# An early pair's epsilon: added by ScalarE as the bias of a copy instead of by VectorE in an operation of its own

## The chip, the core and the metric

The kernel runs on one core of a Trainium2 chip. The core has a matrix engine (PE), a vector engine (DVE), a scalar engine (ACT), a general engine (POOL) and a queue engine (SP) that here issues all transfers between the memory of the chip (HBM) and the core's own memory (SBUF). PE writes its results to a second small memory, PSUM, from which DVE and ACT read. Each engine works through its own list of instructions in order, and waits on semaphores where an instruction needs something from another engine.

The metric is the device time of one execution in microseconds (us), taken as the median of several runs. Before the change it is 964.43 us (three runs, 964.29 to 965.21).

## What is computed

Attention with a block-causal mask over 8 batches of 8 heads (576 positions, head size 64), and then a gated MLP on the 4608 rows that it gives, all in float32:

```python
scores = scale * np.matmul(q, k.transpose(0, 1, 3, 2))
scores = np.where(mask, scores, -1000000000.0)      # block_i >= block_j, blocks of 64
scores = scores - np.max(scores, axis=-1, keepdims=True)
attn = np.exp(scores)
attn = attn / (np.sum(attn, axis=-1, keepdims=True) + 1e-09)
x = np.matmul(attn, v)                              # rows: batch and position, columns: head and size
h = (x @ w1) * (x @ w2) @ w3
out = h @ w_out
```

The 1e-9 in the fifth line is what the change is about.

## The kernel before

**Pairs.** The work of the attention is cut into 32 pairs of heads (4 pairs to a batch). A pair has two heads, `j` = 0 and 1, which share the partitions: head 0 has partitions 0 to 63, head 1 has 64 to 127. For each head the scores are made transposed, in five tiles (`s_tile`, L281, PE writes `s`), ACT takes the exponential (L289 for pairs 0 to 3, the **early** pairs; L296 to L301 for the others), and PE multiplies with the values (L321 early, L345 later, both write `x`).

**The shift.** Ahead of a pair's scores the maxima of its score blocks are found (`shift_mask`: PE L206 writes `mx`, DVE L213 reduces it to `m`, PE L217 transposes `m` to `mt`, ACT L219 writes `ms` with the sign turned). A small transfer (L228) puts `ms` as an extra row into the operand `qk`, one for each head. So the second half of every score tile waits for that transfer. `mt` and `ms` of pair 4 are made while pair 3 is still at work.

**Operands.** `prep_qk` puts the two heads' queries and keys into `qk`, each split into a high and a low part: ACT casts the high part (L251), a transfer copies it to the other partitions (L255), DVE subtracts to get the low part (L258).

**Row sums of an early pair.** The values of an early pair (`ve`) have 64 columns of ones beside the values, so the product `x` holds the row sums on the other head's partitions. ACT copies these out of PSUM to `sm` (L370) and the values to `x32` (L371). `norm` then has a short chain on DVE: reduce `sm` with a transpose to `rr` (L381), add 1e-9 (L382), take the reciprocal (L383), spread it by a transpose to `rb` (L385), multiply into `xr` (two pieces, L392). `rr` has 128 x 18 elements. The later pairs add 1e-9 in another place (`total`, L364), which stays as it is.

**Weights.** Beside pairs 0 to 3 the kernel prepares the weights of the MLP. They arrive as 20 tiles of 1 MB that hold float64 numbers; ACT (L168) and DVE (L169, L170, L171) assemble float32 from them, and for `w1` and `w2` ACT and DVE split each into a high and a low part (L184, L185). PE multiplies `w3` with `w_out` once (`gen_product`, L461), and ACT and DVE split that product (L464, L465). Three buffers `wraw` take the tiles.

**Later stage.** From pair 4 on the attention and the MLP run side by side: ACT casts `xr` to `xh` (L405), POOL makes the rest `xl` (L406), PE multiplies (L481, L499).

**What sets the order.** The first instructions, and all of PE's from pair 4 on, stand in the order in which the code is written. For the rest, and for all engines during pairs 0 to 3, a scheduler orders each engine's list when the kernel is built, with costs of its own for every instruction. So a change of one operation in the early pairs can move others that it has nothing to do with. All lists are fixed once the kernel is built.

Of the kernel before, what the change touches and what calls it, by code (L numbers as in the profile page):

```python
# [7 lines left out]
F32 = mybir.dt.float32  # L8
# [3 lines left out]
AF = mybir.ActivationFunctionType  # L12
# [4 lines left out]
P = 128  # L17
# [60 lines left out]
def block_causal_attention__then__gated_mlp_kernel(ctx, tc, qkv, consts, ident_in, w1, w2, w3t, wout, out_t):  # L78
    nc = tc.nc
    w1, w2, w3t, wout = (w.bitcast(I32) for w in (w1, w2, w3t, wout))  # L80

    cpool = ctx.enter_context(tc.tile_pool(name="cpool", bufs=1))
# [24 lines left out]
    tl = {}  # L107
# [5 lines left out]
    def load_qk(n):  # L113
        t = raw_pool(n).tile([P, RQK], F32, tag="rqk", name=f"rqk{n}")
        for cols in (slice(S, 2 * S), slice(0, S)) if n == 0 else (slice(0, RQK),):
            nc.sync.dma_start(out=t[:, cols], in_=qkv[n // NPAIR, n % NPAIR][:, cols])
        rqk_of[n] = t

    def load_v(n):
        t = raw_pool(n).tile([P, RV], F32, tag="rv", name=f"rv{n}")  # L120
        nc.sync.dma_start(out=t, in_=qkv[n // NPAIR, n % NPAIR][:, RQK:])
        rv_of[n] = t
# [3 lines left out]
    start.enter_context(tc.manual_schedule(engines={ET.PE, ET.DVE, ET.Activation, ET.SP, ET.Pool}))  # L126
    load_qk(0)
    nc.gpsimd.memset(qd, 0.0)
    nc.sync.dma_start(out=both, in_=ident_in)
    load_v(0)  # L130
    wstack = ExitStack()
# [234 lines left out]
    def take_early(n, j, xps, x32, rr):  # L366
        o, x = own[j], oth[j]
        if j == 0:
            tl["sm"] = work.tile([P, S], F32, tag="tr", name=f"sm{n}")
        nc.scalar.copy(tl["sm"][o], xps[x, 384:960])  # L370
        nc.scalar.copy(x32[o], xps[o, 384:960])  # L371

    def take(n, j, xps, x32):
# [5 lines left out]
    def norm(n, x32, rr):  # L379
        if n < EARLY:  # L380
            nc.vector.tensor_reduce(rr, tl["sm"].rearrange("p (b c) -> p b c", c=32), axis=AX.X, op=ALU.max, apply_transpose=True)  # L381
            nc.vector.tensor_scalar_add(rr, rr, 1e-9)  # L382
        nc.vector.reciprocal(rr, rr)  # L383
        rb = work.tile([P, S], F32, tag="tr", name=f"rb{n}")
        nc.vector.transpose(rb, rr.unsqueeze(2).broadcast_to([P, S // 32, 32]))  # L385
        b, c = divmod(n, NPAIR)
        for k in (b, b + 1):
            lo, hi = max(k * TB, b * S), min((k + 1) * TB, (b + 1) * S)
            if (k, c) not in x_of:
                x_of[k, c] = xpool.tile([P, TB], F32, tag=f"x{c}", name=f"xr{k}_{c}")  # L390
            sl = slice(lo - b * S, hi - b * S)
            (nc.vector if n < EARLY else nc.gpsimd).tensor_tensor(out=x_of[k, c][:, lo - k * TB : hi - k * TB], in0=x32[:, sl], in1=rb[:, sl], op=ALU.mult)  # L392
        done_x.add((b, c))
        split_ready()
# [4 lines left out]
    def split_ready():  # L399
        k = st["free"]  # L400
        for c in range(NC):
            if "xh" in tl and k < NTB and (min(k, B - 1), c) in done_x and (k, c) not in st["split"]:
                st["split"].add((k, c))
                src = x_of[k, c]
                nc.scalar.copy(tl["xh"][c], src)  # L405
                nc.gpsimd.tensor_tensor(out=tl["xl"][c], in0=src, in1=tl["xh"][c], op=ALU.subtract)  # L406
# [133 lines left out]
    def pair(n):  # L540
# [9 lines left out]
        for j in range(2):  # L550
# [4 lines left out]
            for step in (FIRST_PLANS[n] if n < len(FIRST_PLANS) else PLAN)[j].split():  # L555
# [6 lines left out]
                with tc.high_priority(offset=0) if early else nullcontext():  # L562
                    if step == "S":
                        s_tile(n, j, next(tiles), p_early)
                    elif step == "F":
                        fill(mlp, 1)
                    elif step == "M":
                        fill(masks, 1)
                    elif step == "A":
                        fill(next_qk, 1)  # L570
                    elif step == "B":
                        fill(own_qk, 1)
                        steps_b += 1
                        if steps_b == 2 and n >= EARLY and not last:
                            load_qk(n + 1)
                    elif step == "V":
                        fill(pvs, 1)
                    elif step == "R":
                        sums(n, j, part)
                    elif step == "N" and early:  # L580
                        take_early(n, j, xps, x32, rr)
                    elif step == "N":
                        take(n, j, xps, x32)
                    elif step == "T":
                        if not early:
                            total(n, part, rr)
                        norm(n, x32, rr)
                    elif step == "Q" and not last:
                        if n + 1 != NPAIR:
                            prep_v(n + 1, j)  # L590
                        if j == 1 and n + 2 <= EARLY:
                            load_qk(n + 2)
                        if j == 1 and n + 2 < NN and n + 1 != NPAIR:
                            load_v(n + 2)
# [66 lines left out]
```

## Time and profile before

| | |
|---|---|
| median of 3 runs | 964.43 us (964.29 to 965.21) |
| the profiled execution's own time | 962.94 us |
| its span, first to last instruction | 961.2 us |
| ACT copies of `sm` (L370) in it | 8, of 626 to 638 ns |
| ACT copies of `x32` (L371) | 8, of 632 to 636 ns |

The profile is of one execution. Its first part gives the busy time of each engine and its share of the span. A timeline row gives start and duration in us, engine, line, operation, what it writes and reads, the shape, how many instructions were merged (x), and in brackets how long the engine had been idle before it and what ended that. "SPq" is the queue engine issuing a transfer. Where instructions follow each other closely the printed durations overlap by some hundredths. A table of stretches gives, for each stretch of time, the busy time of each engine with the number of its instructions, then the clock that PE was granted (1.00 is full speed), the busy share of the DMA engines and what they moved.

### The profile page before, as it was taken

The numbers are of one execution on the slowest core, as the hardware profiler recorded it, in microseconds if no ns is written. First come the engines' busy times: TensorE is split into PE (matmuls) and PEld (weight loads), VectorE is DVE, ScalarE is ACT, GpSimd is POOL, SyncE is SP. The second block draws the span as 40 slices with busy tenths as digits, with TensorE's granted clock in tenths as the row PEclk, the third lists the DMA queues.
The fourth block names the chain that finished last, engine by engine and source line by source line (L and its number), as shares of the span: only waits on it lengthen the run. The fifth ranks groups of instructions, "written<-read, shape, count | busy, mean of one in ns | idle before, by whom it ended". The sixth has DMA issues, their size and how long they took to land.

```text
span 961.2 us, 13354 instructions
## 1 busy us (share of the span) xinstructions
PE 937.1 (97%) x4580; PEld 749.9 (78%) x4608; DVE 609.5 (63%) x1289; ACT 565.9 (59%) x1274; POOL 304.5 (32%) x254
## 2 busy tenths in 40 slices
PE   5999979999999999999999999999999999999998
PEld 3455557888888888888888888888888888888886
DVE  6999977766776677766776777667776776210010
ACT  5776766666666666666666666666666665222121
POOL 0000043442335334533453334333443443223120
PEclk9999979999999999999999999999999999999999
DMA  8897334445445544455445544554455442000001
GB/s 256 299 285 237 108 79 94 114 118 142 113 113 124 145 113 113 113 146 124 111 94 143 124 105 107 135 132 106 106 130 129 106 111 60 22 1 33 12 1 44
DMA packets 48823, 111.68 MB, mean 116 GB/s; under 512 B 5866, under 2 KB 14186, under 8 KB 48756
## 3 DMA queue, kind: packets, MB, share of 16 engines
q1 hardware_dynamic: 48756, 110.84, 44.7%
q8 instruction: 36, 0.59, 0.3%
q14 instruction: 31, 0.25, 0.1%
HBM read 50.51 MB, written 9.44 MB: 62 GB/s over the span
## 4 chain that ended last, share of the span: by engine, by line
PE 90%; DVE 3%; ACT 3%; DMA 2%; issue 1%; POOL 0%; SPq 0%; ACTq 0%; DVEq 0%
PE ab L481 42%; PE o L499 20%; PE s L281 10%; PE x L345 9%; PE mx L206 3%; PE w L461 3%; PE x L321 2%; DMA rqk<-in_qkv 1%; DMA wraw<-in_w 1%; DVE m L213 1%; DVE wbits L170 0%; ACT qk L251 0%; PE tot L362 0%; DVE qk L258 0%; ACT pe L289 0%
## 5 line engine op out<-in xcount | busy, mean ns | idle before, releaser
L489 POOL TENSOR_TENSOR gl<-a,gh 128x512 fp32r<-128x512 f32 x72 | 93.7, 1301 | 239.3 <-ACT gh L488 236.2
L281 PE MATMUL s<-qk 128*128 128x288 f32 (+4 forms) x768 | 158.8, 312 | 9.5 <-DMA qk<-ms 4.7
L281 PEld LDWEIGHTS s<-qk 128*128 128x128 f32 (+1 forms) x768 | 125.8, 183 | 42.5 <-issue 8.9
L213 DVE TENSOR_REDUCE m<-mx 128x1 f32<-128x512 f32 (+6 forms) x256 | 125.4, 503 | 34.0 <-PE mx L206 26.2
L300 ACT ACTIVATE ph<-s 128x448 fp32r<-128x448 f32 x224 | 85.9, 383 | 70.4 <-PE s L281 63.6
L481 PE MATMUL ab<-xh,w2h 128*128 128x512 f32 x288 | 126.4, 439 | 0.0
L271 POOL TENSOR_TENSOR vs<-rv,vs 128x320 fp32r<-128x320 f32 x56 | 48.9, 874 | 233.4 <-ACT vs L270 233.4
L499 PE MATMUL o<-gh,wh 128*128 128x512 f32 x288 | 117.3, 407 | 0.0
L487 DVE TENSOR_TENSOR a<-ab,a 128x512 f32<-128x512 f32 x72 | 49.6, 688 | 106.6 <-PE ab L481 103.9
L302 DVE TENSOR_TENSOR pl<-s,ph 128x448 fp32r<-128x448 f32 x168 | 81.4, 484 | 54.9 <-ACT s L301 54.3
L481 PE MATMUL ab<-xh,w1h 128*128 128x512 f32 x288 | 114.5, 397 | 0.1
L298 DVE TENSOR_TENSOR pl<-rsum,ph 128x288 fp32r<-128x288 f32 x112 | 56.7, 530 | 90.4 <-ACT ph L297 90.2
L481 PE MATMUL ab<-xl,w2h 128*128 128x512 f32 x288 | 113.3, 393 | 0.0
L481 PE MATMUL ab<-xl,w1h 128*128 128x512 f32 x288 | 113.3, 393 | 0.0
L481 PE MATMUL ab<-xh,w1l 128*128 128x512 f32 x288 | 113.0, 392 | 0.0
L499 PE MATMUL o<-gl,wh 128*128 128x512 f32 x288 | 112.9, 392 | 0.0
L481 PE MATMUL ab<-xh,w2l 128*128 128x512 f32 x288 | 112.6, 391 | 0.0
L499 PE MATMUL o<-gh,wl 128*128 128x512 f32 x288 | 112.6, 391 | 0.0
L243 POOL TENSOR_TENSOR rqk<-rqk,hf 128x1152 fp32r<-128x1152 f32 x27 | 72.2, 2673 | 90.8 <-ACT hf L240 90.8
L303 DVE TENSOR_TENSOR rsum<-s,rsum 128x448 f32<-128x448 f32 x224 | 92.7, 414 | 1.7
L345 PE MATMUL x<-ph,vs 128*128 128x128 f32 x336 | 87.2, 312 | 0.0
L301 ACT ACTIVATE s<-s 128x448 f32<-128x448 f32 x224 | 85.1, 380 | 0.0
(76 smaller groups left out, 1730.9 us busy)
## 6 DMA issues: line engine op xcount, KB each, us to landing
qk<-hf SPq DMA_DIRECT2D x108, 288.0 KB, 3.1
rqk<-in_qkv SPq DMA_DIRECT2D x31, 576.0 KB, 4.7
qk<-rqk SPq DMA_DIRECT2D x54, 288.0 KB, 4.8
rv<-in_qkv SPq DMA_DIRECT2D x32, 320.0 KB, 2.9
out_t<-o SPq DMA_DIRECT2D x36, 256.0 KB, 2.0
wraw<-in_w3t SPq DMA_DIRECT2D x8, 1024.0 KB, 5.6
wraw<-in_w SPq DMA_DIRECT2D x8, 1024.0 KB, 6.7
wraw<-in_wout SPq DMA_DIRECT2D x4, 1024.0 KB
```

Of the source, the lines that this page charges most:

```text
L213: nc.vector.reduce_max(m[:, col : col + 1], sc, axis=AX.X)
L243: nc.gpsimd.tensor_tensor(out=lo, in0=rqk_of[n], in1=hf, op=ALU.subtract)
L281: nc.tensor.matmul(t[ks, at : at + q1 - q0], qk[j][:, 2 + s, kr], qk[j][:, s, q0:q1], start=(s == 0), stop=(s == 1))
L298: nc.vector.tensor_tensor(out=low, in0=r, in1=h, op=ALU.subtract)
L300: nc.scalar.activation(h, sc, AF.Exp, scale=SCALE)
L301: nc.scalar.activation(sc, sc, AF.Exp, scale=SCALE)
L302: nc.vector.tensor_tensor(out=low, in0=sc, in1=h, op=ALU.subtract)
L303: nc.vector.tensor_tensor(out=r, in0=sc, in1=r, op=ALU.add)
L345: nc.tensor.matmul(xps[:, to : to + w], v[:, c, :], parts[s][:, a : a + w], start=(u < 2 and s == 0), stop=((u, s) in ((0, 1), (len(PV) - ...
L481: nc.tensor.matmul(acc[i], l[:, c, fs], r[c], start=(c == 0 and s == 0), stop=(c == NC - 1 and s == 2))
L489: nc.gpsimd.tensor_tensor(out=gl[f // 4][:, f % 4], in0=a32, in1=gh[f // 4][:, f % 4], op=ALU.subtract)
L499: nc.tensor.matmul(t, l[:, f, es], r[f // 4][:, f % 4], start=(f == 0 and s == 0), stop=(f == NF - 1 and s == 2))
```

## The change

ScalarE's copy of the row sums becomes an activation with the identity function and a bias, which is a column of a small tile `eps` that POOL fills with 1e-9 at the start. VectorE's addition in `norm` is gone. The copies are 8 (two for each early pair), the additions were 4.

```diff
     nc.gpsimd.memset(qd, 0.0)
+    eps = cpool.tile([P, 32], F32, name="eps")
+    nc.gpsimd.memset(eps, 1e-9)
     nc.sync.dma_start(out=both, in_=ident_in)
...
         if j == 0:
             tl["sm"] = work.tile([P, S], F32, tag="tr", name=f"sm{n}")
-        nc.scalar.copy(tl["sm"][o], xps[x, 384:960])
+        nc.scalar.activation(tl["sm"][o], xps[x, 384:960], AF.Identity, bias=eps[x, 0:1])
         nc.scalar.copy(x32[o], xps[o, 384:960])
...
             nc.vector.tensor_reduce(rr, tl["sm"].rearrange("p (b c) -> p b c", c=32), axis=AX.X, op=ALU.max, apply_transpose=True)
-            nc.vector.tensor_scalar_add(rr, rr, 1e-9)
         nc.vector.reciprocal(rr, rr)
```

No instruction is added or lost beside these and POOL's one memset; the scheduler, however, puts the early pairs' instructions into another order from the end of pair 0 on. Line numbers of the changed kernel are higher by 2 from the second memset to `norm`, and by 1 behind it. From pair 4 on all five lists hold the same instructions in the same order as before, but for what is shown here and for ACT's cast of pair 3's `xr` to `xh`, which now stands behind pair 4's first two exponentials instead of ahead of them. Three places show what moved. In the rows below, numbers in a name are those of the tile, or tell the head (`s_1`) and the pair's turn.

The first place is DVE's list at the end of pair 0, where its chain `rr` stands among the assembly of weights. Before:

```order
L171 SCALAR_TENSOR_TENSOR wo_112<-wraw,wbits 128x1024
L169 TENSOR_SCALAR wbits<-wbits 128x1024
L382 TENSOR_SCALAR rr_185<-rr_185 128x18
L258 TENSOR_TENSOR qk_87<-rqk_173,qk_87 64x1152
L170 SCALAR_TENSOR_TENSOR wbits<-wraw,wbits 128x1024
L465 TENSOR_TENSOR wl<-w_204,wh 128x512
L171 SCALAR_TENSOR_TENSOR w_334<-wraw,wbits 128x1024
```

The same place of DVE's list in the changed kernel:

```order
L173 SCALAR_TENSOR_TENSOR wo_114<-wraw,wbits 128x1024
L171 TENSOR_SCALAR wbits<-wbits 128x1024
L384 RECIPROCAL rr_187<-rr_187 128x18
L172 SCALAR_TENSOR_TENSOR wbits<-wraw,wbits 128x1024
L386 STREAM_TRANSPOSE rb_378<-rr_187 128x576
L466 TENSOR_TENSOR wl<-w_206,wh 128x512
L173 SCALAR_TENSOR_TENSOR w_336<-wraw,wbits 128x1024
```

The reciprocal has moved up, some 10 instructions ahead of where it stood, and the spreading transpose with it; the subtraction for `qk_87` (L258, pair 1's second head) has moved out of this piece, to a place some 17 instructions later.

The second place is ACT's list at the end of pair 3, where the last exponentials of the early stage (`pe`), the cast of pair 4's second head (`qk_87`), pair 3's copies (`sm`, `x_3`), pair 4's shift (`ms`) and its values (`vs`) follow each other. Before:

```order
L184 CAST w2h_89<-wbits 128x1024
L289 ACTIVATE pe_1_843<-s_1_878 128x192
L289 ACTIVATE pe_1_843<-s_1_878 64x64
L251 CAST qk_87<-rqk_730 64x2x576
L370 COPY sm_834<-x_1_842 64x576
L371 COPY x_3_761<-x_1_842 64x576
L219 ACTIVATE ms_903<-mt_901 9x128
L270 CAST vs_934<-rv_732 128x5x64
```

The same place of ACT's list in the changed kernel:

```order
L186 CAST w2h_89<-wbits 128x1024
L291 ACTIVATE pe_1_842<-s_1_855 128x448
L291 ACTIVATE pe_1_842<-s_1_868 128x320
L291 ACTIVATE pe_1_842<-s_1_877 128x192
L291 ACTIVATE pe_1_842<-s_1_877 64x64
L221 ACTIVATE ms_902<-mt_900 9x128
L253 CAST qk_87<-rqk_730 64x2x576
L372 ACTIVATE sm_833<-x_1_841,eps 64x576
L373 COPY x_3_760<-x_1_841 64x576
```

`ms` now stands ahead of the cast of `qk_87` and of both copies, where it stood behind all three; and the cast of the weights `w2h` stands ahead of two exponentials that it stood behind. SP's list follows: the transfers of pair 4's `ms` into both heads' operands now come ahead of the copy of `qk_87` (L257), which stands behind the loading of the next values.

The third place is PE's list at the same time: the last products of pair 3 (`x_1`), pair 4's transpose `mt`, and the first scores of pair 4 (`s_0`). Before:

```order
L206 MATMUL mx_5_893<-kb_796,qd 128x64
L281 MATMUL s_0_962<-qk_86 128x288
L321 MATMUL x_1_842<-pe_1_843,ve_170 128x192
L321 MATMUL x_1_842<-pe_1_843,ve_170 128x64
L217 MATMUL mt_901<-ident,m_800 9x128
L281 MATMUL s_0_962<-qk_86 128x288
L481 MATMUL ab<-xh_926,w1h_80 128x512
```

The same place of PE's list in the changed kernel:

```order
L283 MATMUL s_1_877<-qk_87 64x64 x2
L219 MATMUL mt_900<-ident,m_799 9x128
L283 MATMUL s_0_960<-qk_86 128x288
L323 MATMUL x_1_841<-pe_1_842,ve_172 128x192
L323 MATMUL x_1_841<-pe_1_842,ve_172 128x64
L283 MATMUL s_0_960<-qk_86 128x288
L482 MATMUL ab<-xh_924,w1h_80 128x512
```

The transpose `mt` now stands ahead of pair 3's last two products, where it stood behind them. What follows the second `s_0` is the same in both.

## The prediction

> **What bounds the kernel now.** The page comes first, then a table of stretches: the early stage (24 to 124 us, pairs 0 to 3 beside the weights; the 24 us ahead of it keep their order), the change of stage, and the rest.
>
> ```profile
> span 961.2 us, 13354 instructions
> PE 937.1 (97%) x4580; PEld 749.9 (78%) x4608; DVE 609.5 (63%) x1289; ACT 565.9 (59%) x1274; POOL 304.5 (32%) x254
> ```
>
> ```profile
> 24.00:124.00 100.00, 96.23 (x337) 51.47 (x336) 96.24 (x134) 71.49 (x117) 0.00 (x0) 1.00 0.71 223
> 124.00:134.00 10.00, 4.60 (x13) 3.11 (x12) 9.29 (x10) 6.98 (x16) 7.28 (x6) 0.65 0.44 123
> 134.00:961.00 827.00, 823.28 (x4194) 687.99 (x4221) 487.43 (x1124) 473.56 (x1123) 295.39 (x241) 1.00 0.41 99
> ```
>
> From 134 us on PE is busy 823 of 827 us, and its list is the same in both kernels: what happens earlier shifts that block as a whole. So the question is when PE gets to 134 us. In the early stage DVE and PE are each busy 96 of 100 us. Nearly all that the change touches is there, or in the 10 us behind it, where PE is busy less than half the time and runs at a granted clock of 0.65.
>
> DVE's waits in the early stage are few:
>
> ```profile
> DVE m L213 <- PE mx L206: 1.2, 2, 1.0
> DVE w1l L185 <- ACT w1h L184: 0.8, 1, 0.8
> DVE qk L258 <- ACT qk L251: 0.4, 1, 0.4
> DVE wbits L169 <- ACT wbits L168: 0.4, 2, 0.2
> DVE rr L381 <- ACT sm L370: 0.3, 1, 0.3
> ```
>
> The change of stage is read from the timeline, all engines together:
>
> ```profile
> 123.21 1.15 ACT L251 CAST qk<-rqk 64x1152 fp32r<-64x1152 f32 x1
> 123.70 0.13 DVE L215 TENSOR_REDUCE m<-m 128x1 f32<-128x2 f32 x1
> 124.02 0.28 PE L217 MATMUL mt<-ident,m 128*9 128x128 f32 x1
> 124.27 0.63 ACT L370 COPY sm<-x 64x576 f32<-64x576 f32 x1
> 124.39 1.35 DVE L258 TENSOR_TENSOR qk<-rqk,qk 64x1152 fp32r<-64x1152 f32 x1 [0.56 <-ACT qk L251]
> 124.92 0.63 ACT L371 COPY x<-x 64x576 f32<-64x576 f32 x1
> 125.58 0.27 ACT L219 ACTIVATE ms<-mt 9x128 fp32r<-9x128 f32 x1
> 125.78 0.78 DVE L381 TRANSPOSE_TENSOR_REDUCE rr<-sm 128x18 f32<-128x576 f32 x1
> 125.87 0.82 ACT L270 CAST vs<-rv 128x320 fp32r<-128x320 f32 x2
> 126.40 1.68 POOL L271 TENSOR_TENSOR vs<-rv,vs 128x320 fp32r<-128x320 f32 x2 [124.00 <-ACT vs L270]
> 126.59 0.70 DVE L382 TENSOR_SCALAR rr<-rr 128x18 f32<-128x18 f32 x1
> 127.33 0.27 DVE L383 RECIPROCAL rr<-rr 128x18 f32<-128x18 f32 x1
> 127.63 0.78 DVE L385 STREAM_TRANSPOSE rb<-rr 128x576 f32<-128x576 f32 x1
> 128.04 5.63 POOL L406 TENSOR_TENSOR xl<-xr,xh 128x512 fp32r<-128x512 f32 x4
> 128.25 0.61 PE L281 MATMUL s<-qk 128*128 128x288 f32 x1 [3.95 <-DMA qk<-ms]
> 128.51 2.57 DVE L392 TENSOR_TENSOR xr<-x,rb 128x512 f32<-128x512 f32 x2
> 129.51 0.66 PE L481 MATMUL ab<-xl,w1h 128*128 128x512 f32 x1
> 131.16 2.83 DVE L298 TENSOR_TENSOR pl<-rsum,ph 128x288 fp32r<-128x288 f32 x2
> 134.05 0.74 PE L345 MATMUL x<-pl,vs 128*128 128x448 f32 x1 [0.97 <-DVE pl L298]
> ```
>
> PE idles 3.95 us until the transfer of `ms` has landed (128.25), and its last wait of all is for the second `pl` of DVE, at **134.05**. DVE reaches `pl` through its own chain (L258, L381, L382, L383, L385, `xr`), without a pause. So what ends last at the change of stage is DVE's chain, not the transfer.
>
> **What the change removes.** Four additions. Their group, and a pair of `xr` from the middle of the stage for comparison:
>
> ```profile
> L382 DVE TENSOR_SCALAR rr<-rr x4: 157/170/703, 41.9 to 126.6; 128x18 f32<-128x18 f32 x4
> 106.85 0.82 DVE L392 TENSOR_TENSOR xr<-x,rb 128x512 f32<-128x512 f32 x2
> ```
>
> Three take about 0.17 us each, together at most 0.5 us of a DVE that is 96% busy. The last one took 0.70 us, and its successor started 127.33 - 126.59 = 0.74 us after it. It lay beside POOL's `vs` (126.40 to 128.08); a pair of `xr` likewise took 2.57 us beside POOL's `xl`, against 0.82 us without POOL. So the long time was a wait for POOL, and it goes with the instruction: **-0.74 us** on DVE's chain.
>
> **What it adds.** Eight copies get a bias. The trace has no copy with a bias column; the nearest row is the same copy without one (0.63 us, at 124.27). I take nothing for the bias: per element the same work. The bounds are zero and the whole copy again, 0.63 us, of which only pair 3's second copy can lie on the last chain. ACT is busy 71 of 100 us in the stage, so the other seven are covered; without that cover they would cost as many times the same. POOL's memset lies at the start, where POOL has nothing to do until 126.40; the first copy needs it some 20 us later.
>
> The Trainium skill speaks against the change here: "ScalarE: Activation LUTs", section "What ACT_TABLE_LOAD costs", says that an operand which points to a column of 128 values adds about 93 ns to an activation. As an estimate from that page this is eight times 0.09 us on ACT and 0.09 us on the last chain; the sum would be 0.1 us higher. No run here shows it yet.
>
> **What it moves, in the middle of the stage.** The order rows of the first place put `wl` (L465) right behind the transpose.
>
> ```profile
> 41.88 0.16 DVE L382 TENSOR_SCALAR rr<-rr 128x18 f32<-128x18 f32 x1
> 43.43 1.23 DVE L170 SCALAR_TENSOR_TENSOR wbits<-wraw,wbits 128x1024 int32<-128x1024 int32 x1
> 43.64 0.59 ACT L464 CAST wh<-w 128x512 fp32r<-128x512 f32 x1
> ```
>
> It would come up at 41.88 + 0.27 + 1.23 + 0.78 (reciprocal, L170, transpose) = 44.16 us by the printed durations, which overlap a little, so at about 43.95, while what it reads is cast until 44.23. So one wait of about 0.3 us is new, beside the 0.5 us that went. Further on others go and come: the waits shown above sum to 3.1 us and can at best all vanish, with the additions -3.6 us; new ones of the largest size shown, 1.0 us, at two places would make +2. ACT carries both risks: casts (`wh`, `w2h`) now stand ahead of exponentials that PE waits for. I take **0** for the middle, since the pieces I can name cancel within 0.2 us.
>
> **What it moves, at the change of stage.** ACT now does `ms` first. It needs `mt`, which PE ends at 124.30 as before (124.02 plus 0.28; it needs `m`, not PE's products). So `ms` runs at 124.34 instead of 125.58, and the transfer lands **1.24 us earlier**, at about 127.0. But the cast of `qk` (L251), which was over at 124.36, now begins at about 124.6 and ends at about 125.75: **+1.4 us** for DVE's L258, which waits for it, and for all that is queued behind L258 on DVE. With the 0.74 us gone, `xr` starts 0.66 us later than before, at about 129.16. On ACT the copies of `sm` and `x` and then `vs` follow the cast, so `vs` begins at about 127.1, 1.2 us later; POOL's `vs` then ends at 129.3 instead of 128.08 and its `xl` follow. Who gets ahead there decides. If `xr` comes before the first `xl`, the second `pl` ends about 0.66 us later than before. If `xl` comes first, as in this trace, DVE waits for each `xl` in turn, and the whole of POOL's delay, 1.2 us, and about one part of its L406 (5.63/4 = 1.4 us, less what `xr` itself takes) stand in the way: at most +1.9 us. The two starts differ by 0.1 us, so I cannot say which; between 0.66 and 1.9, I take **+1.0 us**, nearer to DVE's own chain, because that is the row that ends last. PE's first scores are earlier by 1.2 us, but it meets `xl` (129.51 before, at 130.6 or later now) and then `pl`, so nothing of that remains. SP's queue: the copy of `qk` now stands behind the loading of values, which waits for POOL's `vs` (about 129.3); it is needed for the second head, whose scores begin beyond 140 us, and the next load behind it slips by under 1 us.
>
> Sum, for the profiled execution: 962.94 us = 961.2 span + 1.7 around it; 0 in the middle, +1.4 - 0.74 + 0.3 for POOL = +1.0, gives 963.9. That execution lay 1.5 us below the median of the runs, so for the median: 964.43 + 1.0 = **965.4 us**.
>
> **The rivals.** The clock matters for two of them:
>
> ```profile
> 123.60:127.00 3.40, 0.70 (x4) 0.38 (x3) 2.78 (x5) 3.33 (x7) 0.60 (x1) 1.00 0.38 84
> 127.00:130.40 3.40, 2.15 (x6) 1.57 (x6) 3.23 (x5) 1.74 (x4) 3.40 (x4) 0.50 0.36 98
> 130.40:133.85 3.45, 2.15 (x7) 1.45 (x5) 3.37 (x3) 2.31 (x7) 3.28 (x3) 0.50 0.55 178
> 133.85:137.25 3.40, 3.20 (x11) 2.87 (x12) 2.10 (x5) 1.89 (x4) 0.00 (x0) 0.50 0.00 0
> 137.25:140.65 3.40, 3.40 (x18) 2.90 (x18) 1.23 (x5) 2.63 (x7) 0.85 (x1) 1.00 0.00 0
> ```
>
> After a stretch with 0.70 us of PE work the clock was halved, for three stretches of 3.4 us; two with 2.15 us of work did not end that, one with 3.20 us did. PE lost half of what lay behind 134.05: (137.25 - 134.05)/2 = 1.6 us.
>
> *Slower: half speed for one stretch more.* If PE's dense work begins 1.0 us later, the stretch that ends at 137.25 holds about 2.2 us of it, no more than those that did not end it. Half speed would last until 140.65: +1.0 and +1.7 = 967.1. It decides where the dense work starts more than about half a microsecond into a stretch; against it, stretches need not lie the same in each run.
>
> *Faster: the clock is not halved.* `mt`, the last products and the early scores break PE's idle time of 3.95 us into pieces. If that keeps the clock up, -1.6 + 1.0 = -0.6: 963.8. Against it: PE then waits for `xl`, so another stretch is as empty.
>
> This is the rule of the Trainium skill, "TensorE: Matmul & The Clock Gate", section "Part 1: The HAM clock gate (the "warmup" mystery)": the clock goes by activity in free-running windows of 3413 ns, one idle window halves it, one busy one restores it. The trace agrees, with three stretches of 3.4 us.
>
> *Faster: the stage ends earlier.* DVE's waits shrink in the new order by more than the new ones add, about 1 of the 3.1 us, while POOL costs nothing: -1.0 - 0.5 + 0.66 = -0.8: 963.6. DVE's 96% speak for it; PE's 96% beside it against.
>
> *No effect at all.* The casts and PE hide both: 964.4; a special case of the forecast.
>
> **How the numbers follow.** Forecast (964.4 to 966.2, with no effect at its low end) 0.55; half speed longer 0.20; clock kept 0.10; stage earlier 0.15. The range 963.2 to 967.2 leaves out about half of the cases that end lowest and the slower rival's upper part. 0.2% is 1.93 us, about what a measurement can tell from no change: faster means below 962.5, slower above 966.4. Faster: the unlikely ends of the last two cases, 0.08; slower: most of the 0.20 and the forecast's upper end, 0.25; within: 0.67.
>
> **What would show it.** Right: `ms` ahead of L251 by about 1.2 us earlier, L258 of pair 4's second head some 1.4 us behind the final `m` more than before, no 0.70 us row in DVE's chain, and PE's last wait for `pl` near 135. Wrong: `pl` no longer the last wait, the clock at 1.00 between 127 and 137 us, or a stage whose end (the final `m`, 123.70 before) moves by more than 1 us either way.

## The result, and the profile after

The changed kernel takes **970.66 us** (median of 6 runs, 968.02 to 973.1), beside 964.66 us for the kernel before in the same comparison (6 runs). The ratio is 1.0068, with a 95% interval from 1.0053 to 1.0083: slower by 6.0 us. The prediction, 965.4 us with a range of 963.2 to 967.2, is missed.

The page of the changed kernel's profiled execution (970.38 us, against 962.94 before) begins:

```profile
span 968.6 us, 13378 instructions
...
PE 944.1 (97%) x4608; PEld 750.2 (77%) x4608; DVE 607.9 (63%) x1285; ACT 566.4 (58%) x1274; POOL 304.3 (31%) x255
```

The span grew by 7.4 us, and PE's busy time by 7.0. The same three stretches as in the prediction, the last one to 968 us, where before it ended at 961 (columns: stretch, length, busy time and instructions of PE, PEld (PE's loading of weights), DVE, ACT and POOL, PE's clock, DMA share, GB/s):

```profile
24.00:124.00 100.00, 95.88 (x336) 50.69 (x335) 96.96 (x132) 72.11 (x118) 0.00 (x0) 1.00 0.70 224
124.00:134.00 10.00, 5.71 (x16) 3.63 (x17) 7.68 (x9) 8.03 (x17) 6.62 (x6) 0.62 0.37 105
134.00:968.00 834.00, 830.89 (x4221) 689.22 (x4221) 487.85 (x1124) 473.15 (x1123) 295.73 (x242) 1.00 0.40 98
```

The third row holds what nobody touched: 4221 weight loads, as before, at full clock but for its start, and PE busy for 830.89 us where it was 823.28. So the loss lies in the part whose list of instructions is the same.

It does not come from a late start. These rows are the change of stage in the changed kernel, from the timeline:

```profile
123.44 0.28 PE L219 MATMUL mt<-ident,m 128*9 128x128 f32 x1
...
123.98 0.25 ACT L221 ACTIVATE ms<-mt 9x128 fp32r<-9x128 f32 x1
...
124.25 1.15 ACT L253 CAST qk<-rqk 64x1152 fp32r<-64x1152 f32 x1
...
125.42 0.73 ACT L372 ACTIVATE sm<-x,eps 64x576 f32<-64x576 f32 x1
125.43 1.36 DVE L260 TENSOR_TENSOR qk<-rqk,qk 64x1152 fp32r<-64x1152 f32 x1 [2.33 <-ACT qk L253]
...
126.10 0.40 PE L283 MATMUL s<-qk 128*128 128x288 f32 x1 [1.11 <-DMA qk<-ms]
126.18 0.63 ACT L373 COPY x<-x 64x576 f32<-64x576 f32 x1
...
127.63 0.27 DVE L384 RECIPROCAL rr<-rr 128x18 f32<-128x18 f32 x1
...
128.81 2.00 DVE L393 TENSOR_TENSOR xr<-x,rb 128x512 f32<-128x512 f32 x2
...
129.03 5.85 POOL L407 TENSOR_TENSOR xl<-xr,xh 128x512 fp32r<-128x512 f32 x4
...
130.79 0.80 PE L482 MATMUL ab<-xl,w1h 128*128 128x512 f32 x1 [1.34 <-POOL xl L407]
...
132.85 0.89 DVE L300 TENSOR_TENSOR pl<-rsum,ph 128x288 fp32r<-128x288 f32 x1 [0.56 <-ACT ph L299]
...
133.80 0.28 PEld L347 LDWEIGHTS x<-pl,vs 128*128 128x128 f32 x1 [0.42 <-DVE pl L300]
```

`ms` runs ahead of the cast of `qk`, pair 4's scores that wait for it come at 126.10 instead of 128.25, and the weight load for the product with the second `pl`, still the last wait of this place, comes at 133.80; the product stood at 134.05 before. PE enters the later stage a little earlier than it did.

What has changed is PE's pace. Behind pair 31 nothing but the MLP is left, and PE runs through its products without a pause. Its groups there in the changed kernel (from 815 to 960 us; columns: line, operation, what is written and read, shapes, count, busy time, mean ns of one, idle time ahead):

```profile
L500 PE MATMUL o<-gl,wh 128*128 128x512 f32 x75 | 29.6, 395 | 0.0
...
L482 PE MATMUL ab<-xl,w1h 128*128 128x512 f32 x64 | 25.3, 395 | 0.0
L482 PE MATMUL ab<-xh,w2l 128*128 128x512 f32 x64 | 25.3, 395 | 0.0
```

The same view of the kernel before:

```profile
L499 PE MATMUL o<-gl,wh 128*128 128x512 f32 x78 | 30.4, 389 | 0.0
...
L481 PE MATMUL ab<-xl,w1h 128*128 128x512 f32 x64 | 24.9, 389 | 0.0
...
L481 PE MATMUL ab<-xh,w2l 128*128 128x512 f32 x64 | 24.9, 389 | 0.0
```

A product is 6 ns longer, 395 instead of 389. Products overlap, so the pace is read from start to start: from one 512-column product to the next it is 226.9 ns before and 233.2 ns after, over some 600 neighbours each in this tail, where before nearly all lie at 226 or 227 ns and after they alternate between about 229 and 238. In the stretch beside the attention it is about 230 before and 232 after. The later stage has 9 groups of 288 such products, 2592 in all. The last 603, behind the attention, take 141.2 us before and 145.0 after, a difference of 603 times 6.3 ns; the stretch from PE's product with the second `pl` to there, with the other 1989, takes 685.9 and 689.8 us, about 2 ns for each. Together 3.8 + 3.9 = 7.7 us. That is the loss.

What the instructions have not in common with those of before is where their operands lie. The tile `eps` takes 128 bytes of each partition in the first pool, and every buffer allocated behind that pool moves up by as much. Places in the built programs, in bytes from a partition's start:

```
                    before    after
w1h0 (weights)        1664     1664
wh   (weights)       34432    34432
xh0  (streamed)     165760   165888
gh0  (streamed)     187264   187392
```

In these products PE loads 128 columns of the weights and streams 512 columns of `xh`, `xl`, `gh` or `gl`. Modulo 256 all four stood at 128 before; the streamed ones are at 0 now. That, as a cause, was a theory, with the order of the instructions as its rival.

### The profile page after: what moved, and what is told of

It is laid out like the page before. It is cut to its first block, busy times and chain, and to the rows that moved or that the text cites. A ratio compares the mean times of both kernels' runs of the same rounds, so it can differ in the third digit from the quotient of the medians.

```text
span 968.6 us, 13378 instructions
## 1 busy us (share of the span) xinstructions
PE 944.1 (97%) x4608; PEld 750.2 (77%) x4608; DVE 607.9 (63%) x1285; ACT 566.4 (58%) x1274; POOL 304.3 (31%) x255
## 4 chain that ended last, share of the span: by engine, by line
PE 91%; DVE 3%; ACT 2%; DMA 2%; issue 1%; POOL 0%; SPq 0%; ACTq 0%
PE ab L482 42%; PE o L500 21%; PE s L283 10%; PE x L347 9%; PE mx L208 4%; PE w L462 3%; PE x L323 1%; DVE m L215 1%; DMA wraw<-in_w 1%; DMA qk<-ms 1%; DVE wbits L172 1%; DVE wbits L173 0%; PE tot L364 0%; DVE wbits L171 0%; PE mt L219 0%
## 5 line engine op out<-in xcount | busy, mean ns | idle before, releaser
L489 ACT CAST gh<-a 128x512 fp32r<-128x512 f32 x72 | 44.4, 617 | 70.3 <-DVE a L488 69.0
```

## The experiments

All times of a group stand beside runs of the kernel before on the same chip. "Distance" is the place of the streamed buffers less that of the weights, modulo 256 bytes. "Pace" is the mean from start to start in the tail. The next three columns come from the profiles: from the transpose `mt` of pair 1 to that of pair 4 (early stage), from there to PE's product with the second `pl` (change of stage), and from that to the span's end; the last is for how long the clock was halved at the change of stage. Ahead of the early stage the profiles differ too: `mt` of pair 1 comes between 39.6 and 41.7 us, and also in kernels with the same lists it varies by as much.

| kernel | median, us | ratio (95%) | distance | pace, ns | early | change | rest | half clock |
|---|---|---|---|---|---|---|---|---|
| before | 964.66 | 1 | 0 | 226.9 | 83.46 | 10.03 | 827.1 | 10.24 |
| after | 970.66 | 1.0068 (1.0053 to 1.0083) | 128 | 233.2 | 82.04 | 10.36 | 834.8 | 10.24 |
| e1_pad128 | 971.76 | 1.0077 (1.0059 to 1.0094) | 128 | 233.3 | 85.45 | 10.01 | 835.6 | 10.24 |
| e2_eps_early | 962.02 | 0.9977 (0.9964 to 0.999) | 0 | 226.9 | 81.79 | 10.36 | 826.8 | 6.83 |
| e3_pad256 | 964.55 | 1.0002 (0.999 to 1.0015) | 0 | 226.9 | 83.85 | 10.03 | 827.6 | 10.24 |
| e4_pad64 | 969.09 | 1.0051 (1.0035 to 1.0068) | 64 | 229.0 | 83.69 | 10.03 | 831.0 | 10.24 |
| e5_after256 | 962.9 | 0.9988 (0.9976 to 1.0001) | 0 | 227.0 | 82.08 | 10.35 | 827.6 | 6.83 |
| e6_all128 | 964.19 | 0.9998 (0.9986 to 1.001) | 0 | 227.0 | 83.37 | 10.03 | 827.7 | 13.65 |
| e7_g128 | 966.46 | 1.0024 (1.0012 to 1.0035) | 0; `g` 128 | 229.2 | 83.67 | 10.02 | 831.0 | 13.65 |
| e8_weights128 | 972.67 | 1.0086 (1.0067 to 1.0106) | 128 | 233.2 | 84.66 | 10.03 | 835.1 | 10.24 |
| e9_no_add | 958.85 | 0.9953 (0.9935 to 0.997) | 0 | 226.9 | 82.46 | 9.30 | 825.2 | 6.83 |
| e10_bias_and_add | 962.55 | 0.9984 (0.9972 to 0.9997) | 0 | 226.9 | 80.66 | 11.57 | 828.4 | 13.65 |
| e11_pad192 | 971.22 | 1.0077 (1.0056 to 1.0098) | 128 | 232.4 | 84.53 | 10.04 | 834.9 | 10.24 |
| e12_eps_early_again | 962.35 | 0.9978 (0.9964 to 0.9993) | 0 | 226.9 | 81.86 | 10.36 | 825.7 | 6.83 |

**Place or order?** The first kernel has the order of before and the tile of the change, which nothing reads; the second has the change, with its tile in the early pool `wp`, where the buffers of the later stage stay as they were (its edit is against the changed kernel).

```diff
+    eps = cpool.tile([P, 32], F32, name="eps")
+    nc.gpsimd.memset(eps, 1e-9)
```

> The kernel before, plus the unused tile of 128 bytes per partition and its memset; all orders are those of before. Placement theory (the tile moves every buffer that is allocated behind it by 128 bytes, and PE's matmuls are slower from there): about as slow as the changed kernel, 970 us, 512-column matmuls of the last stretch 233 ns apart instead of 227. Order theory (the reordered early lists, or PE's one wait fewer, slow the later stage): as before, 964.5 us and 227 ns.

```diff
-    eps = cpool.tile([P, 32], F32, name="eps")
-    nc.gpsimd.memset(eps, 1e-9)
...
     wp = wstack.enter_context(tc.tile_pool(name="wp", bufs=1))
+    eps = wp.tile([P, 32], F32, name="eps")
+    nc.gpsimd.memset(eps, 1e-9)
```

> The changed kernel with the tile in the early pool, so that no buffer of the later stage moves; all orders are those of the changed kernel. Placement theory: about 964.5 us (within 1 us of before, from the change of stage alone), 227 ns. Order theory: 970 us, 233 ns.

The unused tile alone costs what the change costs (1.0077) and gives the slow pace; the change with its tile elsewhere has the old pace and is faster than both kernels. The order is not what made the change slow.

**Which sizes?** The first of these has the unused tile at 256 bytes, the second at 64.

```diff
+    eps = cpool.tile([P, 64], F32, name="eps")
+    nc.gpsimd.memset(eps, 1e-9)
```

> As the first, with a tile of 256 bytes. Placement theory, if what counts is the place modulo 256 bytes: as before, 964.5 us and 227 ns; if any shift or a larger modulus counts: another pace, 964 to 975 us. Order theory: 964.5 us.

```diff
+    eps = cpool.tile([P, 16], F32, name="eps")
+    nc.gpsimd.memset(eps, 1e-9)
```

> As the first, with a tile of 64 bytes. Placement theory, if what counts is the place modulo 64 bytes: as before, 964.5 us; if modulo 128 or more: slower, 967 to 975 us. Order theory: 964.5 us.

A tile of 256 bytes costs nothing, one of 64 costs 4.3 us: the size as such does not count, and the three sizes fit a cost that goes by the remainder modulo 256. So the next kernel is the change with a tile of 256 bytes, all else equal:

```diff
-    eps = cpool.tile([P, 32], F32, name="eps")
+    eps = cpool.tile([P, 64], F32, name="eps")
```

> The changed kernel with its tile for the constant widened from 128 to 256 bytes per partition, in the same pool and in the same order of instructions: the buffers behind it lie as in the kernel before by multiples of 256. If the loss of the change is only its tile's 128 bytes: 227 ns in the tail and 961 to 963.5 us, as with the constant in the early pool (962.0 us). If the early pool had a part in that gain of its own (its buffers lie otherwise there): 964 to 966 us. If the tile's size has nothing to do with it: 970 us.

962.9 us and 227.0 ns: the loss is gone with 128 bytes more. The interval reaches just past 1. The early stage and the clock have the numbers of the kernel with the early pool, so that pool has no part in them.

**Whose place?** Here the kernel before has 128 bytes ahead of everything, so that weights and streamed buffers both move; then 128 ahead and 128 behind the first pool, so that the weights move by 128 and the streamed ones by 256.

```diff
+    pad = cpool.tile([P, 32], F32, name="pad")
     both = cpool.tile([P, 2 * P], F32, name="ident")
...
     nc.gpsimd.memset(qd, 0.0)
+    nc.gpsimd.memset(pad, 0.0)
```

> The kernel before with an unused tile of 128 bytes per partition ahead of everything in the constant pool, so that the weights and the buffers behind them all move by 128 bytes: both lie at multiples of 256 now, and their places relative to each other are those of before. Rows of the runs so far: spacing of 512-column products in the tail 226.9 ns and 964.8 us where the buffers that the products stream lie 128 bytes off a multiple of 256 (before, and moved by 256), 233.2 ns and 971 us where they lie on one (moved by 128). Theory A, it is the place of the streamed operand alone that counts: 233 ns and 970.5 to 972.5 us. Theory B, it is the place of streamed operand and weights relative to each other (what the two reads do to one another): 227 ns and 964.0 to 966.0 us. Theory C, it is the place of the weights alone: can not be, since the weights did not move in the runs so far, unless both count, when a third spacing is seen.

```diff
+    pad = cpool.tile([P, 32], F32, name="pad")
     both = cpool.tile([P, 2 * P], F32, name="ident")
...
     qd = cpool.tile([P, NB, P], BF16, name="qd")
+    pad2 = cpool.tile([P, 32], F32, name="pad2")
...
     nc.gpsimd.memset(qd, 0.0)
+    nc.gpsimd.memset(pad, 0.0)
+    nc.gpsimd.memset(pad2, 0.0)
```

> The kernel before with 128 bytes ahead of everything in the constant pool and 128 more behind it: the weights move by 128 bytes, the buffers that the products stream by 256. The streamed operands lie as before by multiples of 256, the weights do not. Theory A, the place of the streamed operand alone counts: 227 ns in the tail and 964.0 to 966.0 us. Theory B, the place relative to the weights counts: 233 ns and 970 to 973 us. Together with the run that moves both by 128 bytes this tells A from B: each theory makes one of the two slow, and not the same one. If both are slow, the place of each counts.

How many products PE gets through in the same 140 us of the tail (the stretches view, columns as above), first in the kernel before and then in the changed one:

```profile
815.00:955.00 140.00, 139.92 (x624) 115.43 (x623) 15.43 (x27) 29.11 (x51) 28.45 (x23) 1.00 0.05 18
815.00:955.00 140.00, 139.96 (x607) 112.62 (x607) 18.01 (x32) 31.29 (x57) 28.49 (x23) 1.00 0.04 16
```

With both moved:

```profile
815.00:955.00 140.00, 139.92 (x622) 115.41 (x621) 15.06 (x26) 29.11 (x51) 28.43 (x23) 1.00 0.05 17
```

With the weights alone off by 128:

```profile
815.00:955.00 140.00, 139.96 (x610) 112.52 (x609) 18.76 (x33) 31.89 (x59) 28.49 (x23) 1.00 0.04 16
```

622 against 610, beside 624 and 607, at the same clock and with PE busy all the time. Both moved is as before, the weights moved alone is as slow as the change. With the first two kernels these are all four cases: streamed and loaded operand each at 0 or at 128 modulo 256, fast where they are alike and slow where they are not. Theory A (the streamed operand's own place) falls, theory B holds: what counts is how the two operands of a product lie to one another.

**Each product by its own operands?** The kernel before with 128 bytes in the late pool, just ahead of the buffers of `g`; the lists of ACT, POOL and SP differ a little from before.

```diff
+        pad = pool.tile([P, 32], F32, name="pad")
+        nc.gpsimd.memset(pad, 0.0)
```

> The kernel before with an unused tile of 128 bytes in the pool of the late stage, just ahead of the buffers of g: only gh, gl and what lies behind them move by 128 bytes; xh and xl, which the first products (ab) stream, stay. If the cost goes with the place of the operand of each product, only the products o (from gh and gl) slow down: in the tail about 233 ns from start to start for o and 227 ns for ab, and since o's products are about half of the 512-column products of the late stage (some 2500 in all, the whole move cost 6 to 7 us), 967 to 969.5 us. If it goes with something else of the move (the early buffers, the tiles that ScalarE and VectorE write), then 227 ns for both and 964 to 966 us.

Its groups from 815 to 960 us:

```profile
L501 PE MATMUL o<-gh,wl 128*128 128x512 f32 x79 | 31.2, 395 | 0.0
L501 PE MATMUL o<-gl,wh 128*128 128x512 f32 x78 | 30.8, 395 | 0.0
...
L483 PE MATMUL ab<-xl,w1h 128*128 128x512 f32 x64 | 24.9, 389 | 0.0
...
L483 PE MATMUL ab<-xh,w2l 128*128 128x512 f32 x64 | 24.9, 389 | 0.0
```

`o`, whose buffers moved, takes 395 ns as in the changed kernel, and `ab`, whose buffers stayed, 389 as before. The time is 2.3 us longer, a little less than expected: `o` has 864 of the 2592 products, a third and not half as the expectation has it.

**192 bytes.** This was to be the fourth remainder.

> The kernel before with an unused tile of 192 bytes: late buffers move by 192 bytes. So far, spacing in the tail by the move modulo 256 bytes: 0 gives 226.9 to 227.0 ns, 64 gives 229.0, 128 gives 233.2. If the cost goes by the distance between the two places around a circle of 256 bytes, 192 is like 64: 229 ns, 968 to 970 us. If it goes by which of the two lies ahead, 192 is another case: between 227 and 236 ns. If only an odd multiple of 128 is bad and 64 has a cost of its own for rows not aligned to 128, also 229.

The tile of the kernel that ran had 128 bytes, not 192; it is the first kernel once more, and repeats it (1.0077 both times, 232.4 against 233.3 ns). What 192 does was not tried.

**The other part: what the change does without its tile's place.** The kernel with the tile in the early pool again, for a tighter interval:

> The changed kernel with its constant in the early pool once more, for a tighter interval beside the kernel before on the same chip. First time 962.0 us, ratio 0.9977 (0.9964 to 0.999); the same instructions with 256 bytes in the first pool 962.9, ratio 0.9988 (0.9976 to 1.0001). By the rows: 1.5 us less between the mt of pair 1 and of pair 4, 0.33 us more from there to TensorE's product with the second pl, together 1.2 us less, and up to 1.7 us more or less by how long the clock is halved. Expected ratio 0.998 to 0.999, 962.2 to 963.4 us beside 964.4.

0.9978 after 0.9977: without the shift the change gains about 2 us. To see its parts, one kernel has the removal without the bias, the other the bias without the removal; each has an order of its own, so the two do not split the gain cleanly.

```diff
-            nc.vector.tensor_scalar_add(rr, rr, 1e-9)
```

> The kernel before without VectorE's four additions and with plain copies: the 1e-9 of the early pairs is left out. No tile is added, no buffer moves (227 ns in the tail). The scheduler gives it an order of its own: ScalarE's list nearly that of before (36 rows differ), VectorE's and TensorE's not. From pair 1's transpose mt to pair 4's the runs in the order of before took 83.4 to 83.9 us, those in the order of the change 81.8 to 82.1; the additions themselves, from the start of one to that of the instruction behind it, are 0.17, 0.08 and 0.07 us. Theory 'instructions' (the removal gives what it gives, 0.3 us): 83.1 to 83.5 us between the two mt, and 963 to 964.5 us in all. Theory 'order' (what counts is which waits VectorE meets: its 0.9 us for w1h and 0.4 us for sm near 100 us are gone in the order of the change): since ScalarE's list is that of before, the same waits, 83 us or more, or a new set of waits; then nothing near 81.9. If it does come to about 81.9 us here, removal alone brings the gain.

```diff
+    eps = wp.tile([P, 32], F32, name="eps")
+    nc.gpsimd.memset(eps, 1e-9)
...
-        nc.scalar.copy(tl["sm"][o], xps[x, 384:960])
+        nc.scalar.activation(tl["sm"][o], xps[x, 384:960], AF.Identity, bias=eps[x, 0:1])
```

> The kernel before with the bias (the constant in the early pool, late buffers unmoved) and with the four additions kept, so that the 1e-9 of the early pairs is added twice. Again an order of its own, nearer to that of before on VectorE (74 rows differ) than to that of the change (142), on ScalarE near to that of the change (92). Theory 'instructions': the gain between the mt of pair 1 and of pair 4 (1.5 us) comes from the removal and is not here: 83.4 to 83.9 us, and eight longer copies cost 0.1 us each where they show: 964.4 to 965.5 us. Theory 'order': ScalarE's order, with w1h and the copies sm earlier, removes VectorE's waits for them: 82.0 to 82.6 us (0.3 us more than the change), change of stage with ms first and the addition's 0.7 us beside GpSimd again: 962.5 to 964.5 us.

Both expectations missed in part. With the four additions kept, the early stage is shorter still (80.66 us, where "instructions" had 83.4 to 83.9 and "order" 82.0 to 82.6), so it gets shorter without the removal too; without them, with ScalarE's list near the old one, it came to 82.46, below what either theory gave. Each order has waits of its own on DVE, and no rule of mine foretold which. The time of the kernel without the additions, 958.85 us, also lies over 4 us below its expectation of 963 to 964.5. Its profiled execution is 4.3 us shorter than that of before: 0.6 ahead of `mt` of pair 1, 1.0 in the early stage, 0.7 at the change of stage, and 1.9 behind it, where the clock was back at full speed (131.32) before PE's product with the second `pl` (131.69). At the change of stage the rows are clearer. DVE without the addition, in the kernel with plain copies:

```profile
123.30 1.35 DVE L258 TENSOR_TENSOR qk<-rqk,qk 64x1152 fp32r<-64x1152 f32 x1 [0.96 <-ACT qk L251]
124.69 0.78 DVE L381 TRANSPOSE_TENSOR_REDUCE rr<-sm 128x18 f32<-128x576 f32 x1
...
125.50 0.27 DVE L382 RECIPROCAL rr<-rr 128x18 f32<-128x18 f32 x1
...
126.69 2.02 DVE L391 TENSOR_TENSOR xr<-x,rb 128x512 f32<-128x512 f32 x2
126.89 5.90 POOL L405 TENSOR_TENSOR xl<-xr,xh 128x512 fp32r<-128x512 f32 x4
```

And with it, in the kernel with bias and addition:

```profile
126.02 0.64 DVE L384 TENSOR_SCALAR rr<-rr 128x18 f32<-128x18 f32 x1
...
127.41 5.61 POOL L408 TENSOR_TENSOR xl<-xr,xh 128x512 fp32r<-128x512 f32 x4
...
127.88 2.56 DVE L394 TENSOR_TENSOR xr<-x,rb 128x512 f32<-128x512 f32 x2
```

Without it DVE goes from the start of L258 to that of `xr` in 3.39 us instead of 4.12: the addition's whole 0.73 us. The change of stage takes 9.30 us instead of 10.03, and that this is 0.73 too is chance: L258 begins 0.54 us later behind `mt` (122.39) than before, and the way from `xr` to PE's product is 0.54 us shorter (5.00 instead of 5.54), since `xr` is ahead of POOL's first `xl`. With it, in the other kernel, `xr` comes behind POOL's first `xl` and is 2.56 us long; the change of stage takes 11.57, 1.21 us more than with the bias alone.

## Why the prediction was wrong

**The step that failed** is the one that ended the argument before it began: "From 134 us on PE is busy 823 of 827 us, and its list is the same in both kernels: what happens earlier shifts that block as a whole." The list was the same, the time was not: from PE's product with the second `pl` to the end it is 827.1 us before and 834.8 after, +7.7 of a span that grew by 7.4 (the rest is +0.8 ahead of `mt` of pair 1, -1.4 in the early stage and +0.3 at the change of stage). I read the tile `eps` as an instruction (a memset with nothing beside it) and not as 128 bytes; the experiments show that those bytes alone make the kernel as slow. No rival of mine had it, so no range could. Nor could my signs: those named for being right came, if not in size (`ms` ahead of L251, L258 1.8 us further behind the final `m`, no addition of 0.70 us, PE's last wait for `pl`, at 133.80), but all of them look at the change of stage, and the loss lies in the 830 us behind it.

**The early stage**, taken as 0: -1.4 us (83.46 to 82.04; 81.8 to 82.1 in the four profiles of this order, 83.4 to 83.9 in the five of the old order with a distance of 0 or 64). This is the rival "the stage ends earlier", which put DVE's waits at -1.0 and the three additions at -0.5. DVE's waits from 24 to 124 us in the changed kernel:

```profile
DVE m L215 <- PE mx L208: 0.7, 1, 0.7
DVE wbits L171 <- ACT wbits L170: 0.5, 2, 0.3
DVE qk L260 <- ACT qk L253: 0.4, 1, 0.4
DVE wl L466 <- ACT wh L465: 0.2, 1, 0.2
```

Gone are the 0.8 us for `w1h` and the 0.3 for `sm`; the sum is 1.8 us instead of 3.1. The new wait for `wh`, put at about 0.3 us, is 0.2.

**The addition of the last chain**, -0.74 us: right. From the start of L258 to that of `xr` DVE takes 4.12 us before, 3.38 after, and 3.39 in the kernel without additions.

**The order at the change of stage**, +1.4 and +0.3: the second was wrong in sign. L258 begins 0.37 us behind `mt` before and 1.99 after, so the later cast cost 1.62. From `xr` to PE's product with the second `pl` it is 5.54 us before and 4.99 after, -0.55. With the -0.74 the sum is +0.33 instead of +1.0. `xr` came ahead of POOL's first `xl`, by 0.2 us (128.81 and 129.03), which the prediction left open, and took 2.00 us instead of 2.57; the other case happened in the kernel with bias and addition. And DVE's chain was then no longer what ended last: its second `pl` waited 0.56 us for ACT's `ph` (the row at 132.85), and behind that wait stand pair 4's scores and the product `ab`, which PE held until POOL's first `xl` was done (130.79).

**The bias**, taken as nothing: 0.73 us where the copy beside it (L373) takes 0.63. So a copy that becomes an activation with a bias is 0.10 us longer, eight times, one of them on ACT ahead of pair 4's `vs`. Here "ScalarE: Activation LUTs", section "What ACT_TABLE_LOAD costs", of the Trainium skill was the better guide: its 93 ns for an operand that points to a column agree with these rows.

**The clock**: halved for 10.24 us, three stretches of 3.4 us, as before, so neither rival on the clock came true in the changed kernel. Its rows from the stretches view, the first ahead of the halving, the last at its end:

```profile
123.08:126.49 3.41, 2.12 (x11) 1.19 (x9) 1.08 (x2) 2.77 (x6) 0.00 (x0) 1.00 0.01 4
...
129.90:133.32 3.42, 2.53 (x7) 2.10 (x8) 2.86 (x3) 1.74 (x6) 3.42 (x3) 0.50 0.87 237
133.32:136.73 3.41, 3.33 (x13) 2.65 (x12) 2.40 (x5) 1.28 (x4) 1.56 (x2) 0.50 0.33 120
```

The rival "the clock is not halved" had its condition: PE worked for 2.12 us of the stretch instead of 0.70, and that did not keep the clock up. So that it takes an idle stretch to halve the clock, as the prediction has it, does not hold here. In the other three profiles with this order the clock was halved for two stretches only. What counts is the halved time behind PE's product with the second `pl`: 3.2 us before, 2.9 after, 2.4, 2.2 and 1.2 in those three. Half of the difference is lost work, so this explains at most 1.0 us of their gain.

**The forecast without the shift** would still have been off: by the rows -1.4 + 0.3 = -1.1 us and the shorter half clock, by the medians 0.9977 to 0.9988 (962.0 to 962.9 us, below the range), where +1.0 us was forecast.

What stays open: why the pace differs by 6.3 ns in the tail and by only 2 beside the attention; and why the early stage, too, took 84.5 to 85.5 us in the three kernels of the old order with distance 128, where the changed kernel lost nothing there. In the longest of them (e1_pad128) the clock was halved for one stretch of 3.4 us there, at 96.3 us; the two others have no such stretch.

The version that beats both kernels is the change with its constant in the early pool: 962.02 and 962.35 us, against about 964.8 and 970.7. The kernel without the additions is faster still (958.85), but it leaves out the 1e-9.

## What to carry to other kernels

An edit that allocates anything, even 128 bytes, can move every buffer behind it: compare the places of a product's two operands before and after. Here 256 bytes did no harm, nor did a place with none of the later stage's buffers behind it. When a stretch with an unchanged list of instructions gets longer at the same clock, read the mean duration of one instruction in its quietest part; here a pace that changed by 6 ns, with no idle time ahead of the products, pointed at operands and not at waits. And to test an edit's side effect, add the side effect alone (here the unused tile) and the edit without it.

## What the runs showed of the hardware

In this kernel the pace of TensorE's 512-column float32 products goes by how the loaded and the streamed operand lie to one another modulo 256 bytes in a partition: 226.9 to 227.0 ns at a distance of 0 (seven profiles here besides that of before), 229.0 at 64, 232.4 to 233.3 at 128. Moving both together changed nothing. The Trainium skill, "SBUF — State Buffer", section "Who interferes with whom", gives TensorE two independent read ports, for the streamed operand and for the weights, and says that it never waits on anyone; in these runs its pace nevertheless depends on how the two operands lie to one another. That the two reads meet in the memory is my reading; the runs show only the places and the times.

The clock at the change of stage: in all fourteen profiles it was halved behind a stretch of 3.4 us in which PE worked for 0 to 2.1 us. At half speed, stretches with 0.5 to 2.9 us of PE work did not end it, and those with 3.0 to 3.4 us did.
